# Top-k attention and a GELU layer on one core: the scores of two slots in one run of 64x64 tiles, the value sums two slots later

## The chip, the core and the metric

The kernel runs on one core of one Trainium2 chip. A core has a matrix engine (TensorE, "PE" in the profile, with its weight loads shown apart as "PEld"), a vector engine (DVE), a scalar engine (ACT), a general engine (POOL) and a queue engine that issues DMA transfers (SP). Each engine runs its own instructions in order and waits on semaphores for the others. Matrix products land in PSUM, in banks of 512 fp32 columns, of which this kernel uses eight; ACT and DVE read them from there. The metric is the device time of one execution in microseconds (us); lower is better.

## The reference

```python
# attention: q, k, v are (8 batches, 8 heads, 576 rows, 64), fp32
scores = scale * np.matmul(q, k.transpose(0, 1, 3, 2))
kth = np.partition(scores, -32, axis=-1)[..., -32:-31]      # the 32nd largest of a row
scores = np.where(scores >= kth, scores, -1e9)
attn = np.exp(scores - scores.max(-1, keepdims=True))
attn = attn / (attn.sum(-1, keepdims=True) + 1e-9)
x = np.matmul(attn, v)                # then (B,H,S,D) -> (B*S, H*D) = 4608 x 512
# layer: w_in is 512 x 2048, w_out is 2048 x 512
h = x @ w_in
out = (h * (1.0 / (1.0 + np.exp(-1.702 * h)))) @ w_out
```

Every score row keeps its 32 largest entries, a softmax goes over these, and the rows of all heads of a token then go through a two-layer network.

## The kernel before

The attention is cut into 144 *slots*, 18 to a batch. A slot is 128 query rows of two heads (`hp` is the pair of heads), or, for the last 64 rows of the sequence, 64 rows of two pairs of heads; each of its two halves has 576 keys. Four full slots complete a block of 128 tokens for the network, and a block is four *units*: one `hidden` (x times four of the 16 column blocks of `w_in`, into a PSUM bank) and one `project` (the gated result times `w_out`, 28 matmuls of 128 columns that sum in two banks, arranged as seven products of halves). A slot and a unit come at the same rate, one unit to a slot.

The path of slot n is as follows.

- `scores(n)`: eight matmuls on PE in 64x64 tiles. The array is split in four, by the half of its rows (the head, 64 values deep) and the half of its columns (64 query rows). Four matmuls of 288 keys fill four PSUM banks, and the next four take the other 288 keys. All four banks belong to one tile, `score_banks`, named `s_ps`.
- `copy_scores(n)`: ACT copies the banks to SBUF (`sc`), two copies of 576.
- `pair_up(n)`, `topk(n)` inside `find`: DVE takes the larger and the smaller of keys k and k + 288 (`ranked`, reading one half from PSUM and one from `sc`), then four rounds of eight maxima and their removal. `find(m)` pairs up slot m + 1 behind the eighth of its 14 steps, and inverts the row sums of slot m - 1 behind the ninth.
- `bounds` on POOL, `mask` and `exps` on ACT give the masked exponentials `pr` and their sums; `normalize` on POOL multiplies by the inverse; `split` on ACT writes the halves of each word apart, SP stores them in DRAM (`rows`), and `turn_by_dma` brings them back transposed (`pt`).
- `values_of_two`: PE multiplies `pt` of two slots with v, for each slot eight matmuls over 128 keys (in 128x64 tiles, two side by side) and two over the 64 keys that are left, which are 64 deep (in 64x64 tiles). `x_of_two` copies the sums to the block's x on ACT.

Up to slot 24 the steps of all engines are collected and issued by a long list (`ORDER`). From slot 25 on (`COLLECTED`), `steady_pair(n)`, for n = 25, 27 and so on, fixes the order for two slots. On PE a pair is: a project, a hidden, `scores(n+2)`, a hidden, a project, `scores(n+3)`, and the values of slots n - 3 and n - 2. PE thus goes from 128x64 tiles to 64x64 tiles and back twice in a pair. The two banks of the pool `ps_t` serve the hidden units and the value sums in turn. Each hidden result is read by ACT (`tanh`, and a copy because `aside` is true), gated and combined on POOL (`gate`, `combine`), and then projected.

Loads for later batches are put on the slot at which they are due: `FETCH` for q and k, `READY` for `prepare_by_dma` (a copy on ACT named `halves`, a store and a transposing load on SP, whose slot is `TURN` or the list `turns`), `VALUES` for v. `dues(n)` collects what belongs to slots n and n + 1, and `begin(0)`, `begin(1)` and `prepare_some` issue it in the middle of the pair.

Behind the last pair, `last_units` finishes the units that are left, with DVE in the place of POOL.

In the profile nearly every instruction carries line 131 (issued at once) or 133 (issued from the list), since the wrapper class `Engine` calls them; groups are therefore told apart by their tiles: `s_ps` scores, `o` values (`o<-pt,v_e` the 64 keys, `o<-pt,v_l` the rest), `ph` hidden, `po` project.

Of the kernel before, what the change touches and what calls it, by code (L numbers as in the profile page):

```python
# [121 lines left out]
class Engine:  # L122
# [3 lines left out]
    def __getattr__(self, name):  # L126
        do = getattr(self.engine, name)

        def step(*args, **kwargs):
            if self.engines.collected is None:  # L130
                do(*args, **kwargs)  # L131
            else:
                self.engines.collected.append(lambda: do(*args, **kwargs))  # L133

        return step
# [10 lines left out]
def kernel(  # L146
# [79 lines left out]
    score_banks = pool("ps_s", 1, space=PSUM).tile([P, 2, 2, 512], F32, name="s_ps")  # L226
# [153 lines left out]
    def prepare_by_dma(b, hp):  # L380

        t = loaded.pop((b, hp))[3]
        halves = prp.tile([P, 2 * NF + 1, 2, P], U16, name="halves", tag="pr")
        words = t[:].rearrange("p c j d -> p c (j d)").bitcast(U16)
        nc.scalar.copy(out=halves[:], in_=words.rearrange("p c (e h) -> p c h e", h=2))
        rows = apart_qk.tile([2 * (S + TAIL), 2, P], U16, name="qk_rows")

        def write():
            nc.sync.dma_start(
                rows[0 : 2 * S, :, :].rearrange("(c p) h e -> p c (h e)", p=P),  # L390
                halves[:].rearrange("p c h e -> p c (h e)"),
            )
            nc.sync.dma_start(rows[2 * S : 2 * S + TAIL, :, :], halves[TAIL:P, NF, :, :])

        writes.append(write)

        def turn():
            both = new_pair(b, hp)
            nc.sync.dma_start_transpose(
                out=both[:].bitcast(U16), in_=rows[0 : 2 * S + TAIL, :, :].rearrange("c h e -> (c h) e")  # L400
            )

        if b % 2 and hp > 1:
            at(b * PER + TURN, turn)
        else:
            turns.append(turn)
# [40 lines left out]
    def scores(n):  # L447
        b, t, hps = slots[n]
        ps = score_banks
# [3 lines left out]
        for c in range(2):  # L453
            for i, p, rows, cols in parts:
                on = slice(head_at(n, i) * D, (head_at(n, i) + 1) * D)
                nc.tensor.matmul(
                    ps[rows, i, c, 0:HALF],
                    lhsT=qT[b, hps[p]][on, cols],
                    rhs=kT[b, hps[p]][on, FIRST[i] + c * HALF : FIRST[i] + (c + 1) * HALF],
                )  # L460

    def copy_scores(n):
        ps = score_banks
# [7 lines left out]
    def pair_up(n):  # L471

        b = st[n]["sc"][:, :, HALF:S]
        a = score_banks[:, :, 0, 0:HALF]
# [4 lines left out]
    def pair_first():  # L479
# [4 lines left out]
        nc.scalar.copy(out=half(1), in_=score_banks[:, :, 1, 0:HALF])  # L484
        for c, op in enumerate((ALU.max, ALU.min)):
            nc.vector.tensor_tensor(
                out=ranked[0][:, :, c, :], in0=score_banks[:, :, 0, 0:HALF], in1=half(1), op=op
            )
        nc.scalar.copy(out=half(0), in_=score_banks[:, :, 0, 0:HALF])
# [275 lines left out]
    def hidden(into=None):  # L765
# [4 lines left out]
        ph = ps_t.tile([P, G * P], F32, name="ph", tag="tp")[:] if into else both_banks[free_bank()][:]  # L770
# [616 lines left out]

    def last_units():

        hidden(ps_t)  # L1390
# [5 lines left out]
        project_one()  # L1396
# [15 lines left out]
    with tc.manual_schedule():  # L1412
# [8 lines left out]
        for n in range(COLLECTED, N + 2, 2):  # L1421
            steady_pair(n)
# [35 lines left out]
```

## Time and profile before

| | |
|---|---|
| median of three runs | 1362.26 us (1362.2 to 1364.85) |
| the profiled execution | 1363.19 us |
| its span, first to last instruction | 1361.4 us |
| granted TensorE clock | 0.997 |
| PE busy | 1340.3 us, 98% of the span |
| PE weight loads busy | 1200.6 us, 88% |
| DVE busy | 1274.6 us, 94% |
| ACT busy | 1167.5 us, 86% |
| POOL busy | 979.5 us, 72% |
| DMA over the span | 183 GB/s in the mean |

An engine is busy while one of its instructions runs. Each fp32 matmul leaves two records, so 16 records of `s_ps` are the eight matmuls of a slot. Matmuls of different tiles overlap, so the sum of their durations is more than their busy time, and the durations include a latency; what PE does in a stretch is best read from the start of one group to the start of the next. A row of the timeline has the start, the time from the first start to the last end, the engine, line and operation, output and inputs, shapes, count, and in brackets the idle time ahead of it and what ended that.

### The profile page before, as it was taken

To read this page: it belongs to the slowest core of one execution; us is meant where nothing else is said; L and a number is where in the kernel's file an instruction comes from. 1 tells how busy PE (TensorE), PEld (TensorE's weight loads), DVE (VectorE), ACT (ScalarE), POOL (GpSimd) and SP (SyncE) were. 2 spreads that over 40 slices of the span, in tenths; PEclk is the share of its full clock that TensorE was granted. 3 is DMA by queue.
4 is the path that set the end of the run, shared out by engine and by line. 5 is a ranking of instruction groups with operands and counts; after the bars stand their busy time and mean duration, and the time that the engine had idled before them with its cause. 6 is when DMAs were issued, how large, how long until landed. Compare 5 with 4: busy or idle time off the path is not lost.

```text
span 1361.4 us, 54339 instructions
## 1 busy us (share of the span) xinstructions
PE 1340.3 (98%) x22528; PEld 1200.6 (88%) x22528; DVE 1274.6 (94%) x3374; ACT 1167.5 (86%) x1932; POOL 979.5 (72%) x1782
## 2 busy tenths in 40 slices
PE   8999999999999999999999999999999999999998
PEld 6777679999999999999999999899998999999998
DVE  7999999999999999999999999999999999999912
ACT  6999998898999889898889888889888888888841
POOL 4889887777777777777777777777776777777770
PEclk8999999999999999999999999999999999999999
DMA  8545868777987687897889786988899667756540
GB/s 250 164 128 165 199 165 196 195 199 180 227 215 189 174 200 205 204 203 196 204 198 207 177 203 149 227 202 202 195 207 220 186 161 177 187 148 148 147 107 18
DMA packets 532183, 249.28 MB, mean 183 GB/s; under 512 B 463584, under 2 KB 510176, under 8 KB 531936
## 3 DMA queue, kind: packets, MB, share of 16 engines
q1 hardware_dynamic: 531504, 245.51, 74.1%
q8 instruction: 177, 2.90, 0.9%
q14 instruction: 70, 0.57, 0.1%
q10 hardware_dynamic: 432, 0.30, 0.1%
HBM read 46.01 MB, written 104.60 MB: 111 GB/s over the span
## 4 chain that ended last, share of the span: by engine, by line
PE 89%; DVE 5%; ACT 3%; DMA 1%; issue 1%; POOL 1%; SPq 0%; DVEq 0%; ACTq 0%; POOLq 0%
PE ph L131 33%; PE po L131 29%; PE o L131 10%; PE s_ps L131 10%; PE po L133 3%; DVE ranked L133 3%; DVE top L133 2%; PE ph L133 2%; PE s_ps L133 1%; PE o L133 1%; DMA pt<-rows 1%; ACT sc L133 1%; PE tp L133 1%; ACT pr L133 0%; ACT raws L133 0%
## 5 line engine op out<-in xcount | busy, mean ns | idle before, releaser
L131 DVE MAX8 top<-ranked 128x8 f32<-128x288 f32 (+1 forms) x952 | 526.9, 596 | 0.0
L131 PE MATMUL ph<-xT,win 128*64 128x128 f32 x8064 | 464.3, 273 | 0.0
L131 PEld LDWEIGHTS ph<-xT,win 128*64 128x64 f32 x8064 | 441.3, 137 | 25.9 <-issue 22.4
L131 DVE MATCH_REPLACE8 ranked<-top,ranked 128x288 f32<-128x288 f32 x714 | 382.0, 543 | 0.0
L131 ACT COPY sc<-pr 128x2304 uint16<-128x2304 uint16 x120 | 253.6, 2113 | 84.6 <-POOL pr L131 84.6
L131 POOL TENSOR_SCALAR pr<-pr,rden 128x576 f32<-128x576 f32 x240 | 177.2, 749 | 37.4 <-DVE rden L131 37.4
L131 PE MATMUL po<-raws,h 128*64 128x128 f32 x2000 | 194.3, 273 | 0.0
L131 PE MATMUL po<-wout,h 128*64 128x128 f32 x2000 | 194.3, 273 | 0.0
L131 ACT ACTIVATE pr<-sc,low 128x576 f32<-128x576 f32 x240 | 183.0, 767 | 1.4 <-DMA qk_rows<-halves 1.4
L131 POOL TENSOR_SCALAR some<-den 128x2 f32<-128x2 f32 x120 | 26.7, 222 | 210.3 <-ACT pr L131 210.3
L131 ACT ACTIVATE sc<-sc,cut 128x576 f32<-128x576 f32 x240 | 173.8, 778 | 0.1
L131 DVE TENSOR_TENSOR ranked<-s_ps,sc 128x576 f32<-128x576 f32 x236 | 166.6, 748 | 0.2 <-ACT sc L131 0.2
L131 POOL TENSOR_TENSOR th<-th,h 128x512 f32<-128x512 f32 x123 | 157.7, 1282 | 10.3
L131 PE MATMUL po<-wout,th 128*64 128x128 f32 x2064 | 156.5, 273 | 0.0
L131 ACT COPY sc<-s_ps 128x576 f32<-128x576 f32 x234 | 137.9, 642 | 16.3 <-PE s_ps L131 11.8
L131 PE MATMUL s_ps<-qk_t 64*64 64x288 f32 x1872 | 140.5, 415 | 0.0
L131 PEld LDWEIGHTS po<-wout,h 128*64 128x64 f32 x2000 | 126.5, 137 | 0.0
L131 PEld LDWEIGHTS po<-raws,h 128*64 128x64 f32 x2000 | 126.5, 137 | 0.0
L131 PEld LDWEIGHTS po<-wout,th 128*64 128x64 f32 x2064 | 121.3, 137 | 0.0
L131 PE MATMUL o<-pt,v_l 128*64 128x128 f32 (+1 forms) x2144 | 120.7, 266 | 0.0
L131 PEld LDWEIGHTS o<-pt,v_l 128*64 128x64 f32 x2144 | 106.6, 137 | 9.9 <-issue 9.1
L131 POOL TENSOR_TENSOR h<-th 128x128 f32<-128x128 f32 x248 | 114.0, 460 | 0.3
(121 smaller groups left out, 2207.4 us busy)
## 6 DMA issues: line engine op xcount, KB each, us to landing
rows<-sc SPq DMA_DIRECT2D x136, 576.0 KB, 3.9
qk_rows<-halves SPq DMA_DIRECT2D x24, 576.0 KB, 5.1
out_dram<-raws SPq DMA_DIRECT2D x68, 128.0 KB, 3.8
raws<-in_moe_w_in_dram SPq DMA_DIRECT2D x16, 512.0 KB, 4.9
raws<-in_moe_w_out_dram SPq DMA_DIRECT2D x16, 512.0 KB, 3.9
qk_l<-in_q_dram SPq DMA_DIRECT2D x28, 256.0 KB, 4.1
qk_l<-in_k_dram SPq DMA_DIRECT2D x28, 256.0 KB, 4.2
v_l<-in_v_dram SPq DMA_DIRECT2D x4, 1024.0 KB, 7.7
```

The source lines that it names most:

```text
L131: do(*args, **kwargs)
L133: self.engines.collected.append(lambda: do(*args, **kwargs))
```

## The change

`score_banks` becomes two tiles of two banks, one for slots of even number and one for odd. From slot 25 on a new function `joined_pair` takes the place of `steady_pair`:

- The scores of slots n + 2 and n + 3 come in one run. Of each slot the first 512 keys go as four matmuls of 512 columns, one to a bank. The last 64 keys go as four matmuls of 64 columns into the bank `mixed`, where the value sums stand as well.
- The value sums of slots n - 5 and n - 4 (before: n - 3 and n - 2) stand in the same section: first the matmuls over 128 keys, in 128x64 tiles, then those over 64 keys, among the scores in 64x64 tiles. Two matmuls that write `mixed` from different halves of the array's rows may not run at once, so the lower ones wait on a semaphore, `parted`, that the last two upper ones raise; in the built program these two matmuls carry the increments themselves, and no instruction stands between.
- The order on PE is: values, scores and ends of values, project, hidden, project, hidden. In the first pair, n = 25, there are no value sums, and a third project stands ahead of the last hidden. Both hidden units of a pair go to one bank, `unit`.
- ACT copies a slot's scores as 1024 elements and 128 elements, and the value sums of two slots as one copy of 256.
- The transposing loads of a pair, `turn_by_dma(n-3)` and `turn_by_dma(n-2)`, stand behind the joined section. On SP's queue the second one stands behind the store of slot n - 1.
- The loop runs one pair further, and `last_units` uses `unit` and two of the banks of `s_ps` in turn.
- The loads of q and k, their preparation and the loads of v from batch 2 on are due at other slots, and v of the odd batches comes in two parts.

The number of matmuls is the same in both programs, 11296. ACT has 60 copies fewer, SP nine transfers more.

```diff
@@ -223,7 +222,8 @@
     thp = pool("thp", 8)
     apart = pool("apart", 4, space=DRAM)
     apart_qk = pool("apart_qk", 2, space=DRAM)
-    score_banks = pool("ps_s", 1, space=PSUM).tile([P, 2, 2, 512], F32, name="s_ps")
+    ps_s = pool("ps_s", 2, space=PSUM)
+    score_banks = [ps_s.tile([P, 2, 512], F32, name=f"s_ps{c}", tag="s_ps") for c in range(2)]
     ps_t = pool("ps_t", 2, space=PSUM)
     ps_p = pool("ps_p", 1, space=PSUM)
     both_banks = [ps_p.tile([P, 512], F32, name=f"po{i}") for i in range(2)]
@@ -401,7 +401,9 @@
             )
 
         if b % 2 and hp > 1:
-            at(b * PER + TURN, turn)
+            at(b * PER + TURN[hp], turn)
+        elif (b, hp) > (2, 1):
+            at(b * PER + READY[b % 2][hp] + 1, turn)
         else:
             turns.append(turn)
 
@@ -454,24 +455,22 @@
             for i, p, rows, cols in parts:
                 on = slice(head_at(n, i) * D, (head_at(n, i) + 1) * D)
                 nc.tensor.matmul(
-                    ps[rows, i, c, 0:HALF],
+                    score_banks[c][rows, i, 0:HALF],
                     lhsT=qT[b, hps[p]][on, cols],
                     rhs=kT[b, hps[p]][on, FIRST[i] + c * HALF : FIRST[i] + (c + 1) * HALF],
                 )
 
     def copy_scores(n):
-        ps = score_banks
         sc = st[n]["sc"] = scp.tile([P, 2, S], F32, name="sc")
-        for i in range(2):
-            to = sc[:, i, :].rearrange("p (c k) -> p c k", c=2)
-            nc.scalar.copy(out=to, in_=ps[:, i, :, 0:HALF])
+        for c in range(2):
+            nc.scalar.copy(out=sc[:, :, c * HALF : (c + 1) * HALF], in_=score_banks[c][:, :, 0:HALF])
 
     ranked = {}
 
     def pair_up(n):
 
         b = st[n]["sc"][:, :, HALF:S]
-        a = score_banks[:, :, 0, 0:HALF]
+        a = score_banks[n % 2 if n > COLLECTED + 1 else 0][:, :, 0:HALF]
         ranked[n] = rank.tile([P, 2, 2, HALF], F32, name="ranked")
         for c, op in enumerate((ALU.max, ALU.min)):
             nc.vector.tensor_tensor(out=ranked[n][:, :, c, :], in0=a, in1=b, op=op)
@@ -767,7 +766,10 @@
             return
         x = ready[0]
         fs, x.left = x.left[:G], x.left[G:]
-        ph = ps_t.tile([P, G * P], F32, name="ph", tag="tp")[:] if into else both_banks[free_bank()][:]
+        if into is ps_t:
+            ph = ps_t.tile([P, G * P], F32, name="ph", tag="tp")[:]
+        else:
+            ph = both_banks[free_bank()][:] if into is None else into
         for i, f in enumerate(fs):
             for c in range(CC):
                 parts = 1 if x.whole else 2
@@ -951,10 +953,9 @@
 
 
     READY = (-15, -11, -7, -3), (-17, -13, -9, -5)
-    TURN = -3
-    FETCH = (-19, -13, -9, -5), (-19, -15, -11, -7)
+    TURN = {2: -4, 3: -3}
     FETCH_1 = (-11, -6, -5, -4)
-    VALUES = {(0, 1): 0, (2, 3): 2}, {(0, 1, 2, 3): 2}
+    VALUES = {}, {(0, 1, 2, 3): 2}, {(0, 1): 1, (2, 3): 3}, {(0, 1): 3, (2, 3): 3}
     by_slot = dict(enumerate([2, 3, 3, 3, 3, 3, 3, 3, 3, 3, 3]))
     for n in by_slot:
         first = sum(map(len, list(by_slot.values())[:n]))
@@ -971,12 +972,13 @@
     for b in range(1, B):
         for hp in range(NP):
             if b > 1:
-                at(b * PER + FETCH[b % 2][hp], load_both, b, hp)
+                earlier = 2 * ((b, hp) > (2, 1))
+                at(b * PER + (READY[b % 2][hp] - 4 if earlier else (-19, -13)[hp]), load_both, b, hp)
                 if (b, hp) != (2, 0):
-                    at(b * PER + READY[b % 2][hp], prepare_by_dma, b, hp)
+                    at(b * PER + READY[b % 2][hp] - earlier, prepare_by_dma, b, hp)
             else:
                 at(b * PER + FETCH_1[hp], load_both, b, hp)
-        for hps, n in VALUES[b % 2].items():
+        for hps, n in VALUES[b % 2 if b == 1 else b % 2 + 2].items():
             at(b * PER + n, load_v, b, *hps)
     unfinished = []
     early = []
@@ -1385,15 +1387,186 @@
         if live(n + 1):
             bounds(n + 1)
 
+    joined = []
+    def join():
+        for name in ("mixed", "unit"):
+            joined.append(ps_t.tile([P, 512], F32, name=name, tag="tp"))
+    TAILS = 2 * P
+    parted = tc.alloc_semaphore("parted")
+    parts_done = []
...
+    def joined_section(new, held):
+        ends, rest = [], []
+        for s, m in enumerate(held):
+            b, t, hps = slots[m]
+            pt = st[m]["pt"]
+            for p in range(2 if t == NF else 1):
+                cols = slice(p * TAIL, (p + 1) * TAIL) if t == NF else slice(0, P)
+                to = slice(s * P + cols.start, s * P + cols.stop)
+                main, tail = vv[b, hps[p]]
+                for i in range(2):
+                    on, j = slice(i * TAIL, (i + 1) * TAIL), head_at(m, i)
+                    ends.append((i, j, to, tail[on, j, :], pt[on, NF, cols]))
+                for c in range(NF):
+                    for i in range(2):
+                        rest.append((None, head_at(m, i), to, main[:, head_at(m, i), c, :], pt[:, MAIN[i] + c, cols]))
+            st[m].clear()
+        def score(n, i, p, first, count):
+            b, t, hps = slots[n]
+            cols = slice(t * P + p * TAIL, t * P + (p + 1) * TAIL) if t < NF else slice(FULL, S)
+            on = slice(head_at(n, i) * D, (head_at(n, i) + 1) * D)
+            keys = slice(FIRST[i] + first, FIRST[i] + first + count)
+            return qT[b, hps[p]][on, cols], kT[b, hps[p]][on, keys]
+        def last_keys(r):
+            of = [(n, head_at(n, r), p) for n in new for p in range(2)]
+            at = lambda n, i: TAILS + n % 2 * P + i * TAIL
+            return [(r, p, slice(at(n, i), at(n, i) + TAIL), *score(n, i, p, FULL, TAIL)) for n, i, p in of]
+        def first_keys(n, r):
+            i = head_at(n, r)
+            for p in range(2):
+                to = score_banks[n % 2][p * TAIL : (p + 1) * TAIL, i, :]
+                lhsT, rhs = score(n, i, p, 0, FULL)
+                nc.tensor.matmul(to, lhsT=lhsT, rhs=rhs)
+        upper = [x for x in ends if x[0] == 0] + last_keys(0)
+        lower = last_keys(1) + [x for x in ends if x[0] == 1]
+        halves = [x[1] for x in rest + upper + lower]
+        count = iter(range(len(halves)))
+        def mix(parts):
+            for _, j, cols, lhsT, rhs in parts:
+                k = next(count)
+                nc.tensor.matmul(
+                    joined[0][j * D : (j + 1) * D, cols],
+                    lhsT=lhsT,
+                    rhs=rhs,
+                    start=j not in halves[:k],
+                    stop=j not in halves[k + 1 :],
+                )
+        def mark():
+            nc.tensor.drain(fusable=True).then_inc(parted, 1)
+            parts_done.append(None)
+        mix(rest)
+        ahead = max(0, min(2, len(upper) - 2))
+        mix(upper[:ahead])
+        for n in new[:1]:
+            first_keys(n, 1)
+        mix(upper[ahead:-1])
+        mark()
+        mix(upper[-1:])
+        mark()
+        for n in new[:1]:
+            first_keys(n, 0)
+        for n in new[1:]:
+            first_keys(n, 1)
+            first_keys(n, 0)
+        nc.tensor.wait_ge(parted, len(parts_done))
+        mix(lower)
+    def copy_keys(n):
+        sc = st[n]["sc"] = scp.tile([P, 2, S], F32, name="sc")
+        nc.scalar.copy(out=sc[:, :, 0:FULL], in_=main_keys(n))
+    def copy_last_keys(n):
+        nc.scalar.copy(out=st[n]["sc"][:, :, FULL:S], in_=tails(n))
+    def project_next():
+        leave_all()
+        project_one()
+    def turn_due(m):
+        if live(m) and m > COLLECTED - 2:
+            turn_by_dma(m)
+    def joined_pair(n):
+        begin, prepare_some = dues(n)
+        held = [m for m in (n - 5, n - 4) if live(m) and m > COLLECTED - 4]
+        new = [m for m in (n + 2, n + 3) if live(m)]
+        leave_all()
+        if live(n - 1):
+            exponentials(n - 1)
+        if n == COLLECTED:
+            combine()
+        find(n, 8)
+        joined_section(new, held)
+        turn_due(n - 3)
+        tanh(True)
+        for m in new[:1]:
+            copy_keys(m)
+        if held:
+            x_of(held, joined[0][:, 0 : 2 * P].rearrange("p (s r) -> p s r", s=2))
+        for m in new[:1]:
+            copy_last_keys(m)
+        project_next()
+        leave_all()
+        prepare_some()
+        hidden(joined[1][:])
+        if live(n - 1):
+            normalize(n - 1)
+            split(n - 1)
+        turn_due(n - 2)
+        write_all()
+        gate()
+        begin(0)
+        if live(n):
+            bounds(n)
+        combine()
+        merge_some(3)
+        if live(n):
+            mask(n)
+            exps(n)
+        tanh(True)
+        for m in new[1:]:
+            copy_keys(m)
+            copy_last_keys(m)
+        prepare_some()
+        find(n + 1, 8)
+        project_next()
+        if n == COLLECTED:
+            project_next()
+        hidden(joined[1][:])
+        if live(n):
+            normalize(n)
+            split(n)
+        write_all()
+        while turns:
+            turns.pop(0)()
+        begin(1)
+        gate()
+        if live(n + 1):
+            bounds(n + 1)
+        combine()
+        merge_some(3)
+    units_of_tail = []
     def last_units():
 
-        hidden(ps_t)
+        units_of_tail.append(None)
+        k = len(units_of_tail) % 3
+        hidden(joined[1][:] if k == 0 else score_banks[0][:, k - 1, :])
         merge_some(6)
         write_all()
         tanh(False)
         gate()
         combine()
-        project_one()
+        project_next()
         leave_all()
 
     def issue_in_order():
@@ -1418,8 +1591,9 @@
         for n in range(STEADY + 8, COLLECTED, 2):
             steady_pair(n)
         issue_in_order()
-        for n in range(COLLECTED, N + 2, 2):
-            steady_pair(n)
+        join()
+        for n in range(COLLECTED, N + 4, 2):
+            joined_pair(n)
         combine()
         while ready or to_gate or gated or to_combine or to_project:
             last_units()
```

Left out are the same renaming in `pair_first` and in the head of `scores`, the wrapper `Engine`, which now hands back what an engine's call returns, and the two functions `tails` and `main_keys`, which name the parts of `mixed` and of `score_banks` that hold a slot's scores.

More of the change, by code (lines that the diff above doesn't have):

```diff
@@ L130, in step @@
             if self.engines.collected is None:
-                do(*args, **kwargs)
-            else:
-                self.engines.collected.append(lambda: do(*args, **kwargs))
+                return do(*args, **kwargs)
+            self.engines.collected.append(lambda: do(*args, **kwargs))
         return step
@@ L483, in pair_first @@
         half = lambda c: sc[:, :, c * HALF : (c + 1) * HALF]
-        nc.scalar.copy(out=half(1), in_=score_banks[:, :, 1, 0:HALF])
+        nc.scalar.copy(out=half(1), in_=score_banks[1][:, :, 0:HALF])
         for c, op in enumerate((ALU.max, ALU.min)):
             nc.vector.tensor_tensor(
-                out=ranked[0][:, :, c, :], in0=score_banks[:, :, 0, 0:HALF], in1=half(1), op=op
+                out=ranked[0][:, :, c, :], in0=score_banks[0][:, :, 0:HALF], in1=half(1), op=op
             )
-        nc.scalar.copy(out=half(0), in_=score_banks[:, :, 0, 0:HALF])
+        nc.scalar.copy(out=half(0), in_=score_banks[0][:, :, 0:HALF])
     def topk(n):
@@ L1386, in steady_pair, with tails, main_keys @@
             bounds(n + 1)
+    joined = []
[5 more added lines that the diff above has]
+    parts_done = []
+    def tails(n):
+        return joined[0][:, TAILS + n % 2 * P : TAILS + (n % 2 + 1) * P].rearrange("p (i k) -> p i k", i=2)
+    def main_keys(n):
+        return score_banks[n % 2][:]
+    def joined_section(new, held):
+        begun = set()
+        ends, rest = [], []
[62 more added lines that the diff above has]
+        mix(lower)
```

1 line of the change is left out of this document (removed).

## The prediction

> **What bounds the kernel now.** First the page: shares of the engines, and the chain that ended last.
>
> ```profile
> span 1361.4 us, 54339 instructions
> PE 1340.3 (98%) x22528; PEld 1200.6 (88%) x22528; DVE 1274.6 (94%) x3374; ACT 1167.5 (86%) x1932; POOL 979.5 (72%) x1782
> PE 89%; DVE 5%; ACT 3%; DMA 1%; issue 1%; POOL 1%; SPq 0%; DVEq 0%; ACTq 0%; POOLq 0%
> ```
>
> PE carries the chain, but DVE is close behind, and matmul busy time alone does not tell whether PE is held. So next the waits of the two, between 230 and 1300 us (waiter, releaser, total us, times, longest):
>
> ```profile
> PE o L131 <- DMA pt<-rows: 1.1, 1, 1.1
> PEld ph L131 <- issue: 22.4, 51, 0.4
> PEld o L131 <- ACT sc L131: 1.3, 1, 1.3
> PEld po L131 <- issue: 1.1, 1, 1.1
> ...
> DVE rden L131 <- POOL some L131: 16.0, 39, 2.2
> ```
>
> Three single waits of 1.1, 1.3 and 1.1 are all that holds PE, 3.5 us together; the many of 0.4 come from "issue", with nothing behind them. DVE waits in its inversion. Now PE's timeline of one pair, and of the end of the kernel, where hidden and project follow each other with no scores between:
>
> ```profile
> 707.93 3.66 PE L131 MATMUL ph<-xT,win 128*64 128x128 f32 x64
> 711.52 1.20 PE L131 MATMUL s_ps<-qk_t 64*64 64x288 f32 x16
> 712.65 3.71 PE L131 MATMUL ph<-xT,win 128*64 128x128 f32 x64
> 716.20 0.61 PE L131 MATMUL po<-wout,th 128*64 128x128 f32 x8
> 719.35 1.20 PE L131 MATMUL s_ps<-qk_t 64*64 64x288 f32 x16
> 720.37 0.40 PE L131 MATMUL o<-pt,v_e 64*64 64x128 f32 x8
> ...
> 729.15 1.20 PE L131 MATMUL s_ps<-qk_t 64*64 64x288 f32 x16
> ...
> 1326.43 3.66 PE L131 MATMUL ph<-xT,win 128*64 128x128 f32 x64
> 1329.92 0.61 PE L131 MATMUL po<-wout,th 128*64 128x128 f32 x8
> 1332.98 3.23 PE L131 MATMUL ph<-xT,win 128*64 128x128 f32 x56
> ```
>
> From start to start: a pair is 729.15 - 711.52 = 17.63 us. At the end a hidden takes 1329.92 - 1326.43 = 3.49 and a project 3.06. In the pair the hidden ahead of a score takes 3.59, the one behind it 3.55. So an excursion to 64x64 tiles costs 3.59 + 1.13 + 3.55 - 2 x 3.49 = 1.29 us for four rounds of scores. Four rounds themselves are 1.02 from 719.35 to 720.37, some 0.05 of that (3.55 against 3.49) for the first weights, so a round of 288 columns is 0.24 and the four 0.97. The excursion wastes 1.29 - 0.97 = 0.32 us, and a pair has two. The Trainium skill, "TensorEngine Tiling (Array Packing)", Key Properties, says that a change of tiling mode drains TensorE; it gives no price, and the 0.32 is this trace's.
>
> DVE's floor is read where it pairs up, once a slot:
>
> ```profile
> 759.27 1.41 DVE L131 TENSOR_TENSOR ranked<-s_ps,sc 128x576 f32<-128x576 f32 x2
> 768.10 1.41 DVE L131 TENSOR_TENSOR ranked<-s_ps,sc 128x576 f32<-128x576 f32 x2
> 776.73 1.41 DVE L131 TENSOR_TENSOR ranked<-s_ps,sc 128x576 f32<-128x576 f32 x2
> 785.72 1.42 DVE L131 TENSOR_TENSOR ranked<-s_ps,sc 128x576 f32<-128x576 f32 x2
> 794.52 1.41 DVE L131 TENSOR_TENSOR ranked<-s_ps,sc 128x576 f32<-128x576 f32 x2
> ```
>
> The four slots take 8.83, 8.63, 8.99, 8.80: 8.81 in the mean, which is PE's 17.63 for two. The fastest, 8.63, shows what DVE needs without waits: 17.26 a pair. PE sets the pace, and DVE leaves room for 0.37.
>
> **The change part by part.** *PE's stream.* Matmul counts are equal. A 512-column record is 0.24 x 512/288 = 0.43, one of 128 columns 3.49/32 = 0.11 (64 records in two tiles), one of 64 columns 0.055; a matmul is two records. In the joined run the lower half of the rows streams two mains (2 x 0.86), two tails (2 x 0.11) and one end (0.22): 2.16. The upper half has the same. Before: two slots at 0.97 and the ends at 0.22, 2.16. So the stream neither gains nor loses, if the four tiles run independently of each other although their lengths now differ. That case stands in the trace, at the seam of slot 25, where one end goes ahead of four scores:
>
> ```profile
> 241.92 0.27 PE L133 MATMUL o<-pt,v_e 64*64 64x128 f32 x1
> 241.93 0.47 PE L133 MATMUL s_ps<-qk_t 64*64 64x288 f32 x3
> 242.03 0.27 PE L133 MATMUL o<-pt,v_e 64*64 64x128 f32 x1
> 242.14 0.64 PE L133 MATMUL s_ps<-qk_t 64*64 64x288 f32 x5
> ```
>
> The end takes its tile for two records, 0.22. The score of that tile, next in the program, starts only at 242.14, but the three scores behind it in the program had started at 241.93. Each tile keeps an order of its own.
>
> *Excursions.* Before, from slot 27 to 143: 59 scores alone, 58 with ends behind them, and three times ends alone, 120. After: 59 joined sections and three with values alone, 62. So 58 fewer at 0.32: -18.6 us. From below the gain could be nothing, if the joined run brings gaps as long as the saved ones; from above it is 58 x 0.37 = 21.5, where DVE stops it. I take the 18.6, since the rows show both sides of a change; PE then needs 17.31 a pair, DVE 17.26.
>
> *The semaphore.* In the 59 full sections the upper part ends some 1.3 us (1.72 - 0.44) ahead of the lower matmuls that wait for it: nothing. In the last three pairs nothing lies between; the wait then costs a matmul's way to its end, 0.27 by the row at 241.92: +0.8.
>
> *ACT, POOL and the one bank for hidden.* Rows of the timeline, of the groups and of the transfers (us from issue to landing; the last row is that of the loads of `qk_t`):
>
> ```profile
> 737.20 2.13 DVE L131 MAX8 top<-ranked 128x8 f32<-128x576 f32 x4
> 741.67 1.41 DVE L131 TENSOR_TENSOR ranked<-s_ps,sc 128x576 f32<-128x576 f32 x2
> 744.07 1.48 POOL L131 TENSOR_SCALAR pr<-pr,rden 128x576 f32<-128x576 f32 x2 [0.30 <-DVE rden L131]
> 736.79 2.11 ACT L131 COPY sc<-pr 128x2304 uint16<-128x2304 uint16 x1 [0.18 <-POOL pr L131]
> 740.51 1.44 ACT L131 ACTIVATE sc<-sc,cut 128x576 f32<-128x576 f32 x2
> 743.37 0.95 ACT L131 ACTIVATE raws<-po 128x512 f32<-128x512 f32 x2
> L131 ACT COPY sc<-s_ps 128x576 f32<-128x576 f32 x234 | 137.9, 642 | 16.3 <-PE s_ps L131 11.8
> qk_rows<-halves SPq DMA_DIRECT2D x24, 576.0 KB, 5.1
> pt<-rows SPq DMA_TRANSPOSE x102, 5.3
> DMA to landing us min/median/max: 6.2/7.2/9.3
> ```
>
> Let zero be the start of find(n): the last two of the four maxima at 737.20 belong to it, so 738.5, the pair-up starts at 3.1 and ends, by 1.41 for both its operations, at 4.5; normalize is at 5.5, and the inversion 0.3 ahead of it, 5.2. PE's scores of n + 3 need the bank that this pair-up frees, so they start at 4.5 or later, the section ends at 5.8, and the second hidden starts at 5.9 + 3.1 + 3.5 + 3.1 = 15.6. It needs ACT's two reads of `unit`, which follow mask and exps of slot n: find(n) ends at 8.7, POOL's bounds take some 0.7 (an estimate), mask and exps 743.37 - 740.51 = 2.9, the reads about 1 (as the two at 743.37): 13.3, 2.3 early. Where a pair also has the copy `halves` (24 in the kernel, on ACT as long as the 2.1 of a split), it is some 1.1 later, since ACT has 1.0 of idle time there, and still early. The inversion of slot n - 1 at 5.2 needs its exps and POOL's small step, 0.7 + 2.9 + 0.5 = 4.1; that of slot n at 13.8 needs 12.8, or 13.9 with `halves`. Those 0.1 in each of 23 such pairs are 2.3; PE runs behind DVE by an amount that gives some of it back, and I charge +0.8, between 0 and 2.3 and nearer to the pairs without. The copies of 1024 and 128 instead of two of 576 cost between one and two of those (0.6 to 1.3) for the long one and weigh on ACT alone, whose reader, the next pair-up, comes 5 us later: nothing.
>
> *SP.* The second transposing load stands behind the store of slot n - 1: inversion 5.2, normalize at 5.5, split at 7.1, done at 9.1, store issued, load at 9.7, landed 5.3 later, 15.0. The next pair's values of that slot start at 4.5 - 0.9 (first scores) - 0.2 - 0.9 (half the values) + 17.3 = 19.8: 4.8 early, 2.8 with `halves`. The v loads have nine more issues on SP's queue and a shorter time to land; I let them, and the moved q and k loads, cost what the three old waits cost, 3.5 us out and 3.5 in. The first pair has a project for its missing values, and total PE work behind DVE's end is the same: nothing.
>
> *Sum.* 1363.19 (the profiled execution, 0.9 above the median) - 18.6 + 0.8 + 0.8 = 1346.2. I say 1346.
>
> **The rivals.** *DVE keeps its waits.* If 8.81 a slot is DVE's own loop through ACT and POOL and not PE's pace, nothing changes: 1362. For it speaks that the waits recur; against, that 8.63 occurs in every fourth slot and that the pairs' period stays exactly PE's sum. *Half of it*: DVE at 8.72, a pair of 17.44: 58 x 0.19 = 11 less, 1352.
>
> *Late transposing loads, slower.* Both loads now stand close together behind the section. If in the 23 pairs with `halves` the second one needs the 9.3 us of the slowest load of `qk_t`, it lands 4.0 - 2.8 = 1.2 late: 23 x 1.2 = 28, so 1346 + 28 = 1374. It decides from a landing of 2.8 + 17/23 + 5.3 = 8.8 us on; before, loads of `pt` did not come near it, but they were spread.
>
> *Matmuls end in program order, slower.* Then the tails, behind a main that takes 0.86, could not end before it, three mains follow each other in 0.86 steps, and the section takes 2.58: 0.42 more than I count, 0.10 more than is saved, 58 x 0.10: 1369. The rows at 241.93 and 242.14 speak against it. The Trainium skill states this rule ("TensorE: Matmul & The Clock Gate", The mechanism: matmuls start and end in program order, without reordering); by these rows the trace does not agree.
>
> **How the numbers follow.** Under 0.2% (2.7 us) a measurement of this kernel can't tell a change from none. Forecast 0.64, with a range of its own from 1340 (rounded down from DVE's limit of 21.5, or 18.6 and the old waits gone) to 1350; half of it 0.11; no change 0.07; late loads 0.13; program order 0.05. So faster 0.75, same 0.07, slower 0.18. The range from 1340 to 1364 leaves out the slower cases and little below.
>
> **What would show it.** Right: pairs of 17.3 on PE, one run of scores in each, of some 2.3 with its ends; a hidden of 3.49 in the middle of a pair; DVE slots of 8.6 to 8.7 with hardly a wait in the inversion. Wrong: PE's values waiting for `pt`, scores waiting for the pair-up by more than a few tenths, hidden waiting for ACT, or a joined run of 2.6 or more.

## The result and the profile after

The changed kernel takes 1381.43 us (median of four runs, 1380.57 to 1383.88) against 1362.35 us of the kernel before beside it: a ratio of 1.0139, 95% interval 1.0121 to 1.0157. It is slower by 1.4%; the forecast was 1346 us. The profiled execution took 1380.57 us.

The page after, in the same three lines:

```profile
span 1378.8 us, 54100 instructions
PE 1344.2 (97%) x22528; PEld 1209.6 (88%) x22528; DVE 1269.3 (92%) x3369; ACT 1167.6 (85%) x1872; POOL 982.6 (71%) x1788
PE 61%; DVE 19%; ACT 8%; DMA 5%; issue 3%; POOL 3%; SPq 2%; ACTq 0%; DVEq 0%; POOLq 0%
```

No engine works more than 4 us longer than before (PE 1344.2 against 1340.3 us; its weight loads 9 us), but the chain no longer stays on PE: DVE, ACT and DMA hold a third of it. PE's timeline of one pair of slots, from the values of one joined run to the next:

```profile
953.58 1.92 PE L131 MATMUL mixed<-pt,v_l 128*64 128x128 f32 x32
955.42 0.33 PE L131 MATMUL mixed<-pt,v_e 64*64 64x128 f32 x2
...
957.87 0.66 PE L131 MATMUL po<-wout,th 128*64 128x128 f32 x8
...
960.98 3.66 PE L131 MATMUL unit<-xT,win 128*64 128x128 f32 x64
964.48 0.61 PE L131 MATMUL po<-wout,th 128*64 128x128 f32 x8
...
967.53 3.66 PE L131 MATMUL unit<-xT,win 128*64 128x128 f32 x64
971.03 1.92 PE L131 MATMUL mixed<-pt,v_l 128*64 128x128 f32 x32
...
975.36 0.66 PE L131 MATMUL po<-wout,th 128*64 128x128 f32 x8
```

The hidden in the middle takes 964.48 - 960.98 = 3.50. This pair takes 971.03 - 953.58 = 17.45; where nothing waits, a pair takes exactly 17.33 (below), so the step that was to be gained is there: 17.63 - 17.33 = 0.30 a pair. But few pairs reach it. The first and the last of 58 starts of `mixed`:

```profile
267.80 1.92 PE L131 MATMUL mixed<-pt,v_l 128*64 128x128 f32 x32
1288.66 1.92 PE L131 MATMUL mixed<-pt,v_l 128*64 128x128 f32 x32
```

57 pairs take 1020.9 us. At 17.33 they would take 987.8, so 33.1 us are lost in waits (the *excess* from here on); only 12 of the 57 are at 17.33. At the old 17.63 they would take 1004.9: of the 17.4 us between the two spans, 16.0 lie here.

Where the waits are (waiter, releaser, total us, times, longest), after, 230 to 1300 us:

```profile
DVE rden L131 <- POOL some L131: 35.5, 33, 5.7
ACT sc L131 <- DMA rows<-sc: 34.1, 21, 5.7
PEld s_ps L131 <- DVE ranked L131: 31.9, 47, 1.5
...
ACT raws L131 <- DMA out_dram<-raws: 17.5, 20, 1.7
...
ACT sc L131 <- DVE ranked L131: 8.3, 4, 5.5
```

and two of the same view of before:

```profile
ACT sc L131 <- POOL pr L131: 84.4, 96, 2.2
...
ACT sc L131 <- DMA rows<-sc: 3.1, 3, 1.9
```

ACT now waits for two kinds of stores, 34.1 and 17.5 us, where it waited 3.1 before, and DVE's inversion and PE's scores wait more in turn. The largest case, on ACT, SP and DVE:

```profile
551.60 2.11 ACT L131 COPY sc<-pr 128x2304 uint16<-128x2304 uint16 x1 [1.32 <-POOL pr L131]
...
563.44 1.01 ACT L131 COPY sc<-s_ps 128x1024 f32<-128x1024 f32 x1 [5.75 <-DMA rows<-sc]
```

```profile
550.07 0.58 SPq L131 DMA_DIRECT2D v_l<-in_v_dram  x1
550.70 2.38 SPq L131 DMA_DIRECT2D v_e<-in_v_dram  x2
...
556.75 1.36 SPq L131 DMA_DIRECT2D qk_l<-in_k_dram  x2
558.21 0.54 SPq L131 DMA_DIRECT2D rows<-sc  x1
```

```profile
572.10 0.17 DVE L131 RECIPROCAL rden<-some 128x2 f32<-128x2 f32 x1 [4.91 <-POOL some L131]
578.76 1.41 DVE L131 TENSOR_TENSOR ranked<-s_ps,sc 128x576 f32<-128x576 f32 x2
```

`split` ends at 553.7, but ten loads stand ahead of its store on SP's queue; the store is issued at 558.2 and has landed when ACT goes on at 563.4. ACT waits there because `copy_keys` writes a new buffer of `sc`, of which there are four: slot n + 2 takes the one of slot n - 2, free when that store has landed. Behind the copy stand `split`, mask and exps of the next slot, and DVE's inversion comes 4.91 us late. Of the 8.3 us put down to `ranked` 8.1 are of the same kind: these waits, three of the four, end as such a store lands (5.51 of them stand at 886.3, 4 us after a store that went out behind ten loads). So the copy waits for the store 24 times, some 42 us in all.

### The profile page after: what moved, and what is told of

It reads as the page before. It is cut to its first block, busy times and chain, and to the rows that moved or that the text cites. A ratio compares the mean times of both kernels' runs of the same rounds, so it can differ in the third digit from the quotient of the medians.

```text
span 1378.8 us, 54100 instructions
## 1 busy us (share of the span) xinstructions
PE 1344.2 (97%) x22528; PEld 1209.6 (88%) x22528; DVE 1269.3 (92%) x3369; ACT 1167.6 (85%) x1872; POOL 982.6 (71%) x1788
## 4 chain that ended last, share of the span: by engine, by line
PE 61%; DVE 19%; ACT 8%; DMA 5%; issue 3%; POOL 3%; SPq 2%; ACTq 0%; DVEq 0%; POOLq 0%
PE unit L131 21%; PE po L131 20%; PE mixed L131 7%; DVE ranked L131 7%; DVE top L131 6%; PE s_ps L131 5%; DVE ranked L132 3%; PE po L132 3%; DMA out_dram<-raws 3%; DVE top L132 2%; ACT sc L131 2%; PE ph L132 2%; ACT pr L131 2%; SPq L131 2%; DMA rows<-sc 1%
## 5 line engine op out<-in xcount | busy, mean ns | idle before, releaser
L131 PE MATMUL unit<-xT,win 128*64 128x128 f32 x7936 | 454.5, 273 | 4.5 <-ACT h L131 3.7
L131 PEld LDWEIGHTS unit<-xT,win 128*64 128x64 f32 x7936 | 437.1, 137 | 6.0 <-ACT h L131 5.0
L131 ACT COPY sc<-s_ps 128x1024 f32<-128x1024 f32 x117 | 119.7, 1023 | 64.9 <-DMA rows<-sc 34.1
L131 PE MATMUL po<-wout,th 128*64 128x128 f32 x2064 | 159.8, 276 | 0.5 <-ACT raws L131 0.5
L131 PE MATMUL s_ps<-qk_t 64*64 64x512 f32 x936 | 143.8, 605 | 5.3 <-DVE ranked L131 5.1
L131 PEld LDWEIGHTS po<-wout,th 128*64 128x64 f32 x2064 | 118.2, 137 | 10.6 <-issue 9.3
L131 PE MATMUL mixed<-pt,v_l 128*64 128x128 f32 (+1 forms) x2144 | 119.0, 265 | 4.5 <-DMA qk_l<-in_q_dram 2.9
L131 PEld LDWEIGHTS mixed<-pt,v_l 128*64 128x64 f32 x2144 | 111.0, 138 | 5.0 <-DMA qk_l<-in_q_dram 3.1
```

Source lines behind the costliest of these rows:

```text
L131: return do(*args, **kwargs)
```

## The experiments

Times are medians beside runs of the kernel before on the same chip (medians there 1362.4 to 1365.5 us), so ratios compare better than times.

### One wait taken away, then the other

`e_late`: the first new slot's copies go to where the copy stood before the change.

```diff
-        for m in new[:1]:
-            copy_keys(m)
...
-        for m in new[:1]:
-            copy_last_keys(m)
...
             split(n - 1)
+        for m in new[:1]:
+            copy_keys(m)
+            copy_last_keys(m)
```

> One move: the copies of the first new slot's scores (1024 and 128 wide, on ACT) go from right behind tanh to behind split(n - 1), where the copy stood before the change; nothing else differs from the changed kernel (1381.4 us). Theory 1 (the copy waits for a buffer of sc that is free only when the store of slot n - 2 has landed, and ACT, which works in order, holds split, mask and exps behind it): the copy comes some 4 us later, so of its 42.4 us of waiting (34.1 put down to the store, 8.3 to ranked) under 8 us are left, the waits of 5.5 us shrink to 2 at most, and the excess over 17.33 us a pair falls from 33 us to 10 to 14: 1361 us, 1354 to 1367. Theory 2 (SP alone is late: the loads ahead of the store delay the transposing loads and what they feed): nothing of that is touched, 1379 to 1383. Theory 3 (PE and DVE are at one length, 17.33 and 17.26 us a pair, so that any small delay of either costs time, whatever ACT does): the waits on ACT fall as in theory 1, and the time stays over 1375 us.

Measured: 1384.55 us, 1.0131 (1.0105 to 1.0157). The wait for the store falls from 34.1 to 2.9 us as expected, and nothing is gained: theory 1 as it stood has fallen. The time is what theory 3 gave, but theory 3 says that ACT's order does not matter. The trace tells what does. One pair of it (ACT, then DVE, then PE):

```profile
633.93 0.37 ACT L131 COPY xT<-mixed 128x256 f32<-128x256 f32 x1 [2.03 <-PE mixed L131]
634.20 2.12 ACT L131 COPY halves<-qk_l 128x2304 uint16<-128x2304 uint16 x1
636.22 2.11 ACT L131 COPY sc<-pr 128x2304 uint16<-128x2304 uint16 x1
638.23 1.01 ACT L131 COPY sc<-s_ps 128x1024 f32<-128x1024 f32 x1
```

```profile
642.60 0.17 DVE L131 RECIPROCAL rden<-some 128x2 f32<-128x2 f32 x1 [1.07 <-POOL some L131]
...
649.25 1.41 DVE L131 TENSOR_TENSOR ranked<-s_ps,sc 128x576 f32<-128x576 f32 x2
```

```profile
633.68 0.66 PE L131 MATMUL po<-wout,th 128*64 128x128 f32 x8
...
652.17 0.66 PE L131 MATMUL po<-wout,th 128*64 128x128 f32 x8
```

It is a ring. The joined run ends at 633.7; ACT takes xT out of `mixed`, then `halves`, `split`, the copies, mask and exps; 8.9 us after the run's end DVE can invert, 1.07 late; 6.65 us later comes the pair-up that frees the scores' bank, and the next run ends at 652.17, 18.49 us after the first. In this quiet stretch every second pair, those with `halves`, takes 18.50, and those between 17.33. In the changed kernel itself the copies come ahead of xT, in ACT's idle time, and an undisturbed pair with `halves` takes 975.36 - 957.87 = 17.49 by the rows above: hardly more than PE needs, so that any wait of ACT in it is paid.

The ring also shows why nothing was gained. Over 56 pairs, from the end of one run to the end of the next, the 22 pairs with `halves` lose 12.3 us in the change and none is shorter than 17.48; the 34 others lose 19.6. In `e_late` the others lose 11.4, but those with `halves` 25.2, and none of these is shorter than 18.39. What the removed wait gave in some pairs, the copies took in others.

`e_out`: a block's output store goes out at its pair's start.

```diff
         joined_section(new, held)
+        write_all()
         turn_due(n - 3)
```

> One addition: the waiting stores are written once more just ahead of the transposing load of slot n - 3, so that a block's output store goes out at the start of its pair and not behind the pair's first transposing load; nothing else differs from the changed kernel. If the wait of the next block's copy out of po for that store (17.5 us in all, 20 times, at most 1.72) costs time by itself, it goes wholly and 8 to 15 us come back: 1366 to 1373 us. If it lies in the shadow of the copy's wait for its buffer of sc, or of slack on ACT, the wait goes and the time stays: 1378 to 1383. Theory 2 (SP): the store stands ahead of one transposing load that it stood behind before, 1380 to 1383.

Measured: 1375.06 us, 1.0071 (1.0046 to 1.0096), 6.4 us less than the change (9 us by the ratios); the excess is 26.3 us. The wait for the output store is gone, and the other, 34.1 us in the change, has grown:

```profile
ACT sc L131 <- DMA rows<-sc: 47.3, 30, 5.6
```

That is between the two expectations: part of the 17.5 us seems to have lain in the shadow of the other wait.

`e_both` has both edits. 

> Both of the edits above: the copy behind split(n - 1), the output store at the pair's start. Theory 1 with the wait of the copy out of po: hardly any wait of ACT for a store is left (under 8 us of 60), nearly all pairs take 17.33 us, and the time is 1381.4 less most of the 33 us of excess: 1350 us, 1346 to 1357, below the kernel before (1362). Theory 2: 1379 to 1383. Theory 3: over 1372.

Measured: 1381.78 us, 1.0119 (1.0095 to 1.0144). The time lies where theories 2 and 3 put it, but for neither's reason: 29 of 57 pairs take over 18.3 (from run's end to run's end all 22 with `halves` do), as the ring has it, with few waits for stores left (14.1 us).

`e_loads`: loads of q and k behind the second store (`begin` gets a switch for these loads, `both`, and one for the others).

```diff
-        begin(0)
+        begin(0, both=False)
...
             split(n)
+        begin(0, others=False)
```

> One move on SP's queue alone: the loads of q and k that a pair begins in its first half go behind the store of its second half (behind split(n)) and ahead of the stores that wait; the loads of v stay. ACT's program is the changed kernel's. Theory 1: the store that the next pair's copy waits for stands behind up to four issues fewer, about 3 us (2.9 to 4.5 us of issue in the pairs with q and k); where the copy waited up to 2 us in those pairs it waits no longer, the three waits of 5.5 us fall to about 2.5, the waits of the pairs with an output store stay: 20 to 25 us of 42.4 go, the time 1366 us, 1360 to 1372. Theory 2 agrees in sign; it tells apart from theory 3, by which the time stays over 1378. If the later loads themselves come too late for halves (a copy on ACT in the next pair), halves waits for a load in up to 21 pairs and the time goes up instead, 1382 to 1400.

Measured: 1404.53 us, 1.0286 (1.0258 to 1.0314), somewhat beyond what was expected if the loads come too late. Waits that were absent or smaller (245 to 1300 us):

```profile
ACT raws L131 <- DMA out_dram<-raws: 32.1, 26, 2.8
...
ACT halves L131 <- DMA qk_l<-in_k_dram: 17.5, 18, 2.1
```

Late loads now hold ACT at `halves`, and the output store, which goes out behind them, holds it at the copy out of `po`. Moving the crowd within the queue only changes who waits.

### The ring shortened

`e_swap`: `halves` ahead of the copies, where ACT would wait for `mixed`.

```diff
         tanh(True)
+        prepare_some()
         for m in new[:1]:
             copy_keys(m)
...
         leave_all()
-        prepare_some()
         hidden(joined[1][:])
```

> One move in the changed kernel: the copy halves goes from behind the copies of scores and of xT to right behind tanh, ahead of them. The theory by now is a ring: the joined run ends on PE, then ACT copies xT out of mixed and goes on to halves (where there is one), split, mask and exps of slot n; POOL and DVE invert; DVE's next pair-up frees a bank; and with that the next joined run ends. In a pair with halves this ring takes 17.48 us, all but the 17.33 that PE needs, so every wait of ACT in it is paid; it was 18.50 when the copies (1.2 us) were put into it. Theory: halves moves to where ACT otherwise waits, the ring falls by 2.1 us to some 15.4, and the copy that waits for the store of slot n - 2 comes 2.1 us later, when most stores have landed. Of the 33 us of excess over 17.33 a pair some 15 are left (three pairs with the loads of v ahead of the store, the pairs with an output store): 1363 us, 1357 to 1370. If the ring is not it but SP's queue as a whole, the time stays within 3 us of 1381.

`e_swap_out` adds the line of `e_out`. 

> The move of halves, and the waiting stores written once more ahead of the transposing load of slot n - 3 (a block's output store at its pair's start). By the ring: both waits of ACT are out of it but for the three pairs in which the loads of v stand ahead of the store: 1357 us, 1351 to 1363. If the two gains overlap, as little as the better of them alone.

`e_mend` adds to this a `begin` that, in pairs with loads of v, puts the loads of q and k behind `split(n)`. 

> As the one before, and in pairs that load v the loads of q and k go behind the store of the pair's second slot, so that four issues fewer (3 us) stand ahead of it. By the ring: the three waits of 5.5 us, by now 3.4 as halves lies ahead of them, fall to under 1 us, and the pairs are at PE's 17.33: 1351 us, 1347 to 1357, below the kernel before. If PE and DVE at nearly one length keep the pairs from 17.33 whatever ACT does, 1360 or more.

`e_mend_late` adds to this the move of `e_late`. 

> As the one before, with the copies of the first new slot's scores behind split(n - 1). Alone, this move gained nothing (1384.6): it took the wait for the store away and put 1.2 us of copies into the ring. With halves out of the ring there is room for them (17.48 - 2.1 + 1.2 = 16.6, under 17.33): 1350 us, 1347 to 1356, at least as fast as the one before. If the copies at this place cost by something else than the ring (the next pair-up waits for them), 1360 or more.

Measured:

| | us | ratio to before (interval) | excess | pairs at 17.33 |
|---|---|---|---|---|
| the change | 1381.43 | 1.0139 (1.0121 to 1.0157) | 33.1 | 12 |
| `e_late` | 1384.55 | 1.0131 (1.0105 to 1.0157) | 37.8 | 20 |
| `e_swap` | 1374.81 | 1.0061 (1.0043 to 1.0080) | 24.9 | 32 |
| `e_swap_out` | 1370.33 | 1.0030 (1.0015 to 1.0045) | 20.7 | 33 |
| `e_mend` | 1370.51 | 1.0032 (1.0020 to 1.0045) | 23.3 | 31 |
| `e_mend_late` | 1365.89 | 1.0004 (0.9991 to 1.0017) | 22.3 | 34 |

The direction is the expected one, and over half the pairs are at 17.33, but each time missed its expectation by 12 to 20 us. By their times alone, `e_mend` and `e_mend_late` are what the rivals in their expectations gave (1360 or more). Against these rivals speak the pairs at 17.33, and the versions of the next section, which go below 1360. Most of what is left lies in a few places around the loads of v. `e_mend` did nothing beyond `e_swap_out`, and `e_mend_late` shows why, on ACT:

```profile
ACT halves L131 <- DMA qk_l<-in_k_dram: 22.2, 6, 7.4
```

```profile
557.07 2.11 ACT L131 COPY halves<-qk_l 128x2304 uint16<-128x2304 uint16 x1 [7.39 <-DMA qk_l<-in_k_dram]
```

Early in its pair, `halves` now waits for loads that I had made later. The crowd had to leave the pair, not be reordered in it.

### The crowd taken apart

`e_early` is `e_swap_out` with these loads one pair earlier, behind the `halves` that frees their only buffer; `e_early_late` has the late copies too.

```diff
-                at(b * PER + (READY[b % 2][hp] - 4 if earlier else (-19, -13)[hp]), load_both, b, hp)
+                at(b * PER + (READY[b % 2][hp] - (6 if hp == 1 else 4) if earlier else (-19, -13)[hp]), load_both, b, hp)
```

> The changed kernel with halves right behind tanh and the output store at its pair's start (as e_swap_out, 1370.3), and the loads of q and k that fell into a pair with loads of v (those of the second head pair of each batch from the third on) one pair earlier, behind the halves that frees their buffer. In e_swap_out and e_mend nearly all the lost time lies around these pairs: there halves waits for its loads (9.4 and 20.5 us, 6 times) and the copy for its store. By the ring: no wait of halves is left, the store of the crowded pairs goes out 3 us earlier; six places of 2 to 5 us shrink by half: 1358 us, 1352 to 1364. If the pairs that take the loads over (with an output store and the writes of halves) become the crowded ones, the waits only move: 1366 to 1374.

> As e_early, with the copies of the first new slot's scores behind split(n - 1) (against e_mend_late, 1365.9: the q and k loads are one pair earlier in the crowded pairs, not behind the store). By the ring: no wait of halves (22.2 us there), the store has 4 us more to land: 1350 us, 1345 to 1356, below the kernel before. If the waits only move to the pairs that take the loads over: 1362 to 1370.

Measured: 1358.46 us, 0.9963 (0.9947 to 0.9979), and 1353.42 us, 0.9916 (0.9903 to 0.9929): both times lie in their expected ranges, and the second version is 0.8% faster than the kernel before. Lines of the second that answer to those of the change:

```profile
span 1351.1 us, 54140 instructions
```

```profile
ACT xT L131 <- PE mixed L131: 52.9, 39, 3.2
...
ACT sc L131 <- DMA rows<-sc: 19.1, 18, 2.5
DVE rden L131 <- POOL some L131: 14.8, 18, 3.7
...
PEld s_ps L131 <- DVE ranked L131: 8.8, 19, 1.5
```

```profile
265.34 1.92 PE L131 MATMUL mixed<-pt,v_l 128*64 128x128 f32 x32
...
703.27 1.92 PE L131 MATMUL mixed<-pt,v_l 128*64 128x128 f32 x32
720.59 1.92 PE L131 MATMUL mixed<-pt,v_l 128*64 128x128 f32 x32
737.92 1.92 PE L131 MATMUL mixed<-pt,v_l 128*64 128x128 f32 x32
...
1261.22 1.92 PE L131 MATMUL mixed<-pt,v_l 128*64 128x128 f32 x32
```

57 pairs take 995.9 us, 8.1 over 57 x 17.33, and 40 of them are at 17.33. The store is waited for 19.1 us even so; those waits have become cheap, as the small excess shows; `halves` no longer stands in the ring with them (`e_no_swap`, below, tests this). ACT's 52.9 us of waiting for `mixed` show nothing of the kind by themselves: they are 85.1 in the slow `e_late`.

### Two runs against the theory

`e_no_swap` is `e_early_late` with `halves` put back behind xT. 

> The fastest version (e_early_late, 1353.4) with one part undone: halves goes back behind the copy of xT. Stores and loads go as there. By the ring: the pairs with halves go back to 18.50 us as in e_late, 1.17 over 17.33, in some 20 pairs, 23 to 27 us: 1378 us, 1373 to 1383, though hardly a wait for a store is left. If the crowded queue of SP alone was the cause and the place of halves does not matter: 1352 to 1360.

Measured: 1377.58 us, 1.0094 (1.0077 to 1.0110). Its ACT hardly waits for a store, yet 26 of its pairs take over 18.3 (from run's end to run's end all 22 with `halves` do), as the one between these two starts of `mixed` (663.17 - 644.67 = 18.50):

```profile
ACT sc L131 <- DMA rows<-sc: 4.0, 6, 1.7
```

```profile
644.67 1.92 PE L131 MATMUL mixed<-pt,v_l 128*64 128x128 f32 x32
...
663.17 1.92 PE L131 MATMUL mixed<-pt,v_l 128*64 128x128 f32 x32
```

So the place of 23 copies in ACT's order is worth 24 us, with the queue in order.

`e_twice` is the change with each copy `halves` made twice. 

```diff
-        nc.scalar.copy(out=halves[:], in_=words.rearrange("p c (e h) -> p c h e", h=2))
+        for _ in range(2 if joined else 1):
+            nc.scalar.copy(out=halves[:], in_=words.rearrange("p c (e h) -> p c h e", h=2))
```

> The changed kernel with each of the 23 copies halves made twice from slot 25 on (the second writes the same again): 2.0 us more on ACT, in the place that it has there, behind the copies of scores and of xT. By the ring, where such a pair already takes 17.48 us, all of it is paid: 23 x 2.0 = 46, 1427 us (1415 to 1435), and its pairs take 19.5. If ACT has room in these pairs (it is busy 85% of the span, 2.6 us of a pair idle), most of it is hidden: 1381 to 1395.

Measured: 1433.72 us, 1.0506 (1.0489 to 1.0522): 52.3 us more, 2.3 for each copy of 2.0. All of it is paid, as expected, but not where: few pairs take 19.5; mostly two in a row take 18.5. PE's hidden has come to wait for ACT's reading of `unit` too, 34.5 us against 3.7 in the change:

```profile
PE unit L131 <- ACT h L131: 34.5, 24, 3.9
```

In the change ACT is idle 15% of the span, and it has no room at this place.

A fifth buffer of `sc`, which should remove the copy's wait for the store and leave all else in its place, was not tried, so what that wait costs alone stays open. What remains of `e_early_late`'s excess (8.1 us) lies nearly all, 7.0, in pairs with `halves`, and was not followed.

## Why the prediction was wrong

*Excursions, -18.6: right.* It was 0.30 a pair against 0.32, over 58 pairs 17.4, and the joined run was as long as worked out: a pair of 17.33 less two hiddens of 3.50, projects of 3.11 and 3.05 and 1.84 of values leaves 2.33, against "some 2.3". The tiles ran independently. In that, the Trainium skill's rule that matmuls start and end in program order ("TensorE: Matmul & The Clock Gate", The mechanism) again does not agree with the trace: by it the run would have been 0.42 longer. DVE's floor of 8.63 a slot held as well: 59 of 105 slots between 300 and 1250 us take it in the change.

*The semaphore, +0.8: right in size.* The last three joined runs hold values alone; in PE's timeline the lower ends of the first start at 1307.82 after 0.18 of waiting, some 0.5 for three.

*ACT with `halves`, +0.8: too small, and the right place.* The sum found that the second inversion is 0.1 late in such a pair. Undisturbed pairs of this kind take 17.49 in the change, 0.16 over, so 3 or 4 us for 23. The sum should have been read the other way: an inversion that comes 0.1 late means that ACT has no reserve in these pairs, so that whatever else is added to its order there is paid in full.

*The copies, "weigh on ACT alone, whose reader, the next pair-up, comes 5 us later: nothing": the step that failed.* It asked who waits for the copy, and not what the copy itself waits for. Put some 4 us earlier in ACT's order, it comes before the store that frees its buffer has landed, 24 times, and holds `split`, mask and exps behind it: some 42 us of waiting, in the ring. Nor do the copies weigh on ACT alone: where they stood before, they wait for hardly any store (`e_late`), but then they stand in the ring, and a pair with `halves` takes 18.50 instead of 17.49, so that undoing this step by itself gains nothing. What failed with it is the room that the paragraph gave ACT in these pairs. The block's copy out of `po` was not costed at all; it waits 17.5 us for the block's earlier store, and an earlier store alone (`e_out`) was worth 6.4 us.

*SP and the loads, "3.5 us out and 3.5 in": wrong.* The transposing loads did arrive in time, as worked out; PE nowhere waits for `pt`. Of PE's own waits in the change (230 to 1300 us) these are the longest behind 5.1 us for the pair-up:

```profile
PE unit L131 <- ACT h L131: 3.7, 4, 1.8
PE mixed L131 <- DMA qk_l<-in_q_dram: 2.9, 1, 2.9
PE mixed L131 <- DMA v_l<-in_v_dram: 1.5, 2, 0.9
```

The 2.9, put down to a load of q, ends at 881.98, as a load of v lands (881.85), so PE waits 4.4 us for loads of v, three times. The 3.5 counted one old wait twice: the 1.3 of the weights and the 1.1 of the matmul stand both at 1023.2, so PE itself was held 1.9 us, in two places (1.1, and 0.8 with nothing behind it). By PE alone the exchange thus cost up to 2.5 us. The larger part is ACT's: the store also stands on SP's queue, behind up to ten loads, and the prediction followed only the transposing loads. In three places, two of them behind ten loads, it is the copy's wait of some 5.5 us.

*The one bank for hidden, 2.3 early: right only without the waits.* PE waits 3.7 us there in the change, in four places (the first of the lines above).

*Of the rivals*, the slower one by late transposing loads came to 1374, near the result, by a mechanism that did not occur. That a wait of ACT for a store takes the gain was not among them; "hidden waiting for ACT" and scores waiting for the pair-up were named as signs of a wrong forecast, and both are there.

So the excess of 33.1 us, less the 17.1 gained (57 x 0.30), makes the pairs 16.0 us longer. The runs show it from three sides: the ring with the queue in order (`e_no_swap`, 1377.6), the queue crowded with the ring shortened (`e_swap_out`, 1370.3), and both mended (`e_early_late`, 1353.4, 7 us above the forecast).

## What to carry to other kernels

When an instruction is moved ahead in an in-order engine's program, ask what it waits for itself, its output buffer and the store that frees it included, and not only who waits for it; then ask what is queued behind it. Where two engines come within a few tenths of the same length, look for a ring through the third, however idle that engine looks: there a copy of 2 us cost its whole length at one place (`e_twice`) and little at another (`e_early_late`). The crowded queue was mended here by moving transfers to another pair; reordering them within the crowd changed only who waited.

## What the runs showed of the hardware

Nothing that contradicts the traces before, but two sizes that had not been expected. The SP queue took 8 us to issue ten loads (550.07 to 558.21), 0.6 to 1.7 us each. The store behind them went out 4.5 us after its data were ready (553.7 to 558.2) and landed 5.1 us later, so that its place in that queue counted nearly as much as its transfer. And waits for the same store cost very different amounts: 34.1 us of them, by the profile's account, go with a loss of 33.1 in the change, 19.1 with one of 8.1 in `e_early_late`, 2.9 with one of 37.8 in `e_late`; a wait's total in the profile is no price until it is known whether the engine had time to spare there.
